# Unit 0's two chunks share one sine-table window: a new issue order for all engines of a fused gated-attention and MoE kernel

## The chip, the cores and the metric

One core of one Trainium2 chip runs the whole program in one launch. The metric is the device time of one execution in microseconds, median of a few runs. The core has five engines that run side by side, each with its own instruction queue in strict order: PE (TensorE, matmuls), DVE (VectorE), ACT (ScalarE, which needs a table load before it may change between the log/exp functions and the sine functions), POOL (GpSimd) and SP (SyncE, here the only issuer of transfers). An instruction that waits blocks all that stand behind it in its engine's queue.

## The reference, cut to what matters

```python
def _attn_ref(q, k, v, a_re, a_im):            # (4, 8, 768, 48) each
    mag = np.sqrt(a_re * a_re + a_im * a_im)
    scale = np.minimum(mag, 0.999) / (mag + 1e-06)
    a_re_n, a_im_n = a_re * scale, a_im * scale
    for t in range(S):                         # complex decay of a state, per (b, h)
        S_re, S_im = a_re_n*S_re - a_im_n*S_im, a_re_n*S_im + a_im_n*S_re
        S_re = S_re + outer(k[t], v[t])
        y[t] = q[t] @ S_re
    return y

def _moe_ref(x, w_in, w_out):                  # x: 3072 x 384, d_ff 2048
    h = x @ w_in
    sp = log1p(exp(h))                         # h itself above 20
    return (h * np.tanh(sp)) @ w_out
```

The attention output, reshaped to 3072 rows of 384, is the input `x` of the second part.

## The kernel before

**Units and chunks.** The 4 x 768 time steps are cut into 12 units of 256 steps (`UNITS`), each with two chunks of 128 (`NCH`). The complex decay is written in polar form. For each unit ACT and DVE work out the log of the magnitude, add it up along time (a scan, L409), and take exps of plus and minus the sum (L413, L414); the angle goes through an arctan, a second scan (L426), a reduction to one turn (L431 or L432, then L433), and sines (L491). `grow` (L453) multiplies q and k by the exps, `turn1` and `turn2` (L475) by the sine and the cosine, and six transfers per chunk (`relay`, L471) bring the result into the layout of the matmuls (tile `T`). Then PE works on the chunk: transposes of k (`kn`, L561, copied out of PSUM at L562), the 128 x 128 products (`pa`, L597; from unit 3 on `pp`, L592) with their mask (L599), the output (`ypsum`, L612, copied at L617), and the state update (`pd`, L632, then L637 or L639 and L640). The output is moved by transfers (`xf<-y`) and split into a high and a low half (`xH`, `xL`, L255 and L256).

**The second part.** `mm1` (L695 for unit 0, L699 after) multiplies by `w_in` into `ph`, ACT and DVE make the activation (L703 to L709), its result is split into halves (L255, L256), and `mm2` (L732 for unit 0's early half, L736) multiplies by `w_out` into `po`. The weights are loaded as `raw` (SP, L277), converted by ACT (L285), DVE (L287, L288) and POOL (L290) and split into `w` (L255, L256).

**Warming matmuls.** `spin` (L525) issues 84 matmuls into `junk` whose results nobody reads; the first 40 wait for chunk 0's L433 (`turned`), the other 44 for the copy of chunk 0's output (`copied`).

**Order.** The functions are called in the order of a list of due times, which gives each engine a numbered list of instructions. `in_order` then chains them in the order that the table `ORDER` names: in `"Activation": "0 45 47 46 48+3 ..."` the number n is the n-th instruction of that engine in program order, and `48+3` means 48, 49, 50. `FLIP` lists which of 214 movable steps (copies out of PSUM, casts, one reduction step, two small column copies) go to their second engine, and `SETS` gives the number and kind of table loads (`l` log and exp, `t` sine and arctan). A table load is one more numbered ACT instruction, so `ORDER` alone says where it stands. Unit 0 is worked by chunks:

```python
for g in groups:
    steps += each(*(() if g else (size,)), slope, test, mag1, mag2, mag3, mag4, mag5, grow, gs=(g,))
    ...
    steps += [lambda g=g: window((g,)), lambda g=g: turn1(g), lambda g=g: turn2(g)]
```

PSUM tiles of the tag `pa` (`pkn`, `pa`, `pd` of units 1 and 2) share two buffers: a product in `pa` can start only when a transpose's buffer was copied out.

Of the kernel before, what the change touches and what calls it, by code (L numbers as in the profile page):

```python
# [115 lines left out]
    """,  # L116
    "DVE": """
# [72 lines left out]
FLIP = "0 3 5 8 10+2 16 23+3 27 29 31 34 41 43+2 46+6 53+3 57 60+2 63 65+4 70 76+2 81 87+3 92+2 96 98 100 103+6 111+7 119 122 131 135+3 139 142 144 146+2 149 151+3 157 159+3 165+2 169+2 172 175 177+5 184 188+2 191+2 194 196 200+2 203+2 206+4 213"  # L190
# [808 lines left out]
```

## Time and profile before

| what | value |
|---|---|
| median of 3 runs | 567.69 us (567.3 to 569.6) |
| profiled execution | 568.46 us |
| its span (first to last instruction) | 566.8 us |
| mean granted clock of PE | 0.998 |
| busy: PE, DVE, ACT, POOL | 541.2, 467.1, 473.5, 41.1 us |
| matmuls into `junk` | 84, 22.9 us busy |
| table loads | 45, 57.7 us busy |

Busy time is the union of an engine's instructions. The start times of a timeline are microseconds from the first instruction; matmuls overlap in the pipeline, so their pitch (the distance of two starts) is what one costs PE.

### The profile page before, as it was taken

What the parts mean: (1) busy time and instruction counts of PE and PEld (TensorE: products, weight loads), DVE (VectorE), ACT (ScalarE), POOL (GpSimd) and SP (SyncE); (2) the same over time, 40 slices, a digit from 0 to 9 for tenths busy, and PEclk for the clock granted to TensorE, in tenths of its full rate; (3) what the DMA queues carried; (4) which work ended last, traced back from release to release, by engine and by line L of the source; (5) the groups of instructions that cost most, each with busy time, mean ns of one, the idle gap of its engine ahead of it and who ended that gap; (6) DMA issues with size and microseconds to landing.
All of it is one profiled execution on the core that took longest, in us unless ns stands there. A gap on an engine that the chain in (4) does not pass through costs nothing.

```text
span 566.8 us, 14350 instructions
## 1 busy us (share of the span) xinstructions
PE 541.2 (95%) x5830; PEld 504.3 (89%) x5830; DVE 467.1 (82%) x766; ACT 473.5 (84%) x757; POOL 41.1 (7%) x50
## 2 busy tenths in 40 slices
PE   0987999999999999999999999999999999999997
PEld 0556877899999999999999999999999999999996
DVE  6989999999999999899997999687997776563643
ACT  7998999999999999899986998878877689554562
POOL 3122322322000000000000000000000000000000
PEclk9999999999999999999999999999999999999999
DMA  8686763924675738627447426536446414301000
GB/s 290 225 276 167 299 194 90 303 65 105 189 211 131 208 106 226 174 80 212 124 124 190 130 85 178 180 89 178 148 116 156 117 54 118 103 17 43 16 14 32
DMA packets 69063, 81.65 MB, mean 144 GB/s; under 512 B 6144, under 2 KB 60672, under 8 KB 68992
## 3 DMA queue, kind: packets, MB, share of 16 engines
q1 hardware_dynamic: 68992, 80.68, 49.0%
q8 instruction: 47, 0.77, 0.6%
q14 instruction: 24, 0.20, 0.1%
HBM read 45.51 MB, written 11.40 MB: 100 GB/s over the span
## 4 chain that ended last, share of the span: by engine, by line
PE 83%; DVE 6%; DMA 4%; ACT 3%; SPq 2%; issue 1%; DVEq 0%
PE ph L699 32%; PE po L736 31%; PE ypsum L612 7%; PE po L732 4%; PE pp L592 4%; PE pp L632 2%; ACT L239 1%; PE pa L597 1%; PE ph L695 1%; DMA T<-QK 1%; DMA I<-a_im 1%; SPq L471 1%; DVE X L475 1%; DMA T<-X 1%; DVE QK L453 1%
## 5 line engine op out<-in xcount | busy, mean ns | idle before, releaser
L699 PE MATMUL ph<-xH,w 128*128 128x256 f32 x1104 | 222.1, 286 | 0.4 <-DVE g L709 0.4
L736 PE MATMUL po<-w,gh 128*128 128x384 f32 x704 | 202.0, 339 | 0.0
L699 PEld LDWEIGHTS ph<-xH,w 128*128 128x128 f32 x1104 | 179.9, 190 | 3.8 <-issue 1.4
L699 PE MATMUL ph<-xL,w 128*128 128x256 f32 x552 | 156.1, 283 | 0.0
L736 PEld LDWEIGHTS po<-w,gh 128*128 128x128 f32 x704 | 129.6, 188 | 2.3 <-issue 1.7
L736 PE MATMUL po<-w,gl 128*128 128x384 f32 x352 | 118.5, 337 | 0.0
L699 PEld LDWEIGHTS ph<-xL,w 128*128 128x128 f32 x552 | 104.9, 190 | 0.9 <-issue 0.5
L709 DVE SCALAR_TENSOR_TENSOR g<-e,ph 128x512 f32<-128x512 f32 (+1 forms) x100 | 65.8, 659 | 39.1 <-ACT e L707 30.9
L705 ACT ACTIVATE e<-e 128x512 f32<-128x512 f32 (+1 forms) x100 | 60.4, 610 | 29.0 <-DVE e L704 28.9
L703 ACT ACTIVATE e<-ph 128x512 f32<-128x512 f32 (+1 forms) x100 | 57.2, 573 | 31.9 <-PE ph L699 23.0
L736 PEld LDWEIGHTS po<-w,gl 128*128 128x128 f32 x352 | 66.2, 188 | 0.0
L256 DVE TENSOR_TENSOR gl<-g,gh 128x512 fp32r<-128x512 f32 x88 | 60.2, 687 | 6.3 <-ACT gh L255 5.9
L707 ACT ACTIVATE e<-e 128x512 f32<-128x512 f32 (+1 forms) x100 | 60.6, 608 | 1.2
L706 ACT ACTIVATE e<-e 128x512 f32<-128x512 f32 (+1 forms) x100 | 60.2, 608 | 0.7
L239 ACT ACT_TABLE_LOAD x45 | 57.7, 1283 | 1.6 <-PEq L951 0.8
L704 DVE TENSOR_SCALAR e<-e 128x512 f32<-128x512 f32 (+1 forms) x100 | 40.6, 409 | 17.0 <-ACT e L703 16.8
L525 PE MATMUL junk<-cmask 128*128 128x512 bf16 x84 | 22.9, 407 | 15.5 <-DVE I L433 14.7
L290 POOL TENSOR_TENSOR raw<-raw 128x768 int32<-128x768 int32 x16 | 31.5, 1975 | 63.1 <-DVE raw L288 24.5
L255 ACT CAST gh<-g 128x512 fp32r<-128x512 f32 x47 | 28.7, 611 | 6.7 <-PE po L736 5.6
L593 DVE COPY_PREDICATED am<-tmask,pp 128x512 f32<-128x512 uint8 x36 | 26.4, 737 | 7.9 <-PE pp L592 7.8
L612 PE MATMUL ypsum<-T,S 96*48 96x128 f32 x320 | 32.5, 276 | 0.1
L525 PEld LDWEIGHTS <-cmask 128*128 128x128 bf16 x84 | 8.4, 104 | 24.6 <-issue 17.5
(106 smaller groups left out, 828.6 us busy)
## 6 DMA issues: line engine op xcount, KB each, us to landing
T<-X SPq DMA_DIRECT2D x72, 129.0 KB, 2.9
T<-QK SPq DMA_DIRECT2D x72, 129.0 KB, 3.4
raw<-w_in SPq DMA_DIRECT2D x8, 768.0 KB, 6.1
raw<-w_out SPq DMA_DIRECT2D x8, 768.0 KB, 7.2
kd<-vx SPq DMA_DIRECT2D x45, 128.0 KB, 2.8
kn<-kd SPq DMA_DIRECT2D x15, 384.0 KB, 3.3
V<-v SPq DMA_DIRECT2D x12, 384.0 KB, 6.5
out_dram<-o SPq DMA_DIRECT2D x24, 192.0 KB, 2.3
```

The lines of the kernel that those rows point to most:

```text
L239: nc.scalar.preload_act_table_set({"l": "natural_log_exp_and_others", "t": "trig_and_small"}[name])
L256: leng(out=lo, in0=src, in1=h.bitcast(F32), op=ALU.subtract)
L290: nc.gpsimd.tensor_tensor(hi, hi, lo, ALU.add)
L612: nc.tensor.matmul(py[64 * par:64 * par + D, i, :], lhs, rhs, start=n == 0, stop=first or n == 1)
L699: nc.tensor.matmul(ph[:, a, :], rows_in(parts[j][:, wp], kt, a), st[xp][:, kt, :], start=n == 0, stop=n == 8)
L703: act(e, ph, AF.Exp)
L704: nc.vector.tensor_scalar_min(e, e, math.exp(20.0))
L705: act(e, e, AF.Square, bias=1.0)
L706: act(e, e, AF.Ln, scale=0.2, bias=0.2)
L707: act(e, e, AF.Exp, scale=-1.0)
L709: nc.vector.scalar_tensor_tensor(g, e, 2.5, ph, ALU.subtract, ALU.mult)
L736: nc.tensor.matmul(po[t], gp[:, a, tsl], rows_out(parts[NPAIR + j][:, wp], a), start=j in starts and a == 0 and n == 0, stop=j + 1 in ends ...
```

## The change

Only the tables differ; no function is edited. Read through the numbering above, they say this.

- **ACT, unit 0.** Before, the queue goes: log/exp table; the logs and exps of chunk 0 (and two early steps of chunk 1); sine table; arctans and sines of chunk 0; log/exp table; logs and exps of chunk 1; sine table; sines of chunk 1; log/exp table. After, it goes: log/exp table; logs and exps of chunk 0 and of chunk 1, and unit 1's squares, first log and first exp; sine table; arctans of chunk 0, unit 1 and chunk 1; sines of chunk 0; two conversions (L285); the reduction step and the sines of chunk 1; log/exp table. Two loads fewer there. Over the whole program `SETS` goes from 45 loads to 39.
- **DVE and POOL, unit 0.** The logs' DVE steps of chunk 1 now stand before chunk 0's scan of the angle; POOL does the small column copies of chunk 1 and chunk 0 in that order, then the conversions.
- **SP.** Ahead of chunk 0's relay now stand also a third weight load (`raw`, 768 KB) and unit 1's V; chunk 1's relay sends QK before X; unit 1's QK loads and chunk 0's `xf` transfers alternate; two `w_out` loads now stand between the relays of unit 1's two chunks.
- **PE.** 34 instead of 28 junk matmuls ahead of chunk 0's first transpose, 12 together between unit 0's last two products; 73 instead of 75 in all ahead of unit 1's first `pa`. There, unit 1's `pa` is followed by one `mm1` group and then the second `pa` (before: both `pa`, then the `mm1` group). Later, the order of the groups is new everywhere.
- **Engines of movable steps** (90 of 214 change): 29 casts go from ACT to DVE and 26 from DVE to ACT; 6 copies of `y` to DVE and 3 to ACT, among these chunk 0's (DVE before, ACT after) and chunk 1's the other way; of unit 1's first two `kn` copies the second goes from DVE to ACT, behind a table load and an arctan; 8 column copies from DVE to POOL and 4 back; 6 output copies to ACT and 3 to DVE. ACT has 746 instructions before and 736 after, DVE 738 and 738, POOL 47 and 51, PE 4333 and SP 384 in both.

```diff
 ORDER = {
     "PE": """
-        0+28 40+8 28 48+4 29+5 52+4 64+16 56+8 34 80 35 81+2 124+4 83+4 36 87+6 128+4 93+8 37 101+2 132+4 103+2 38 105+3
...
+        0+34 40+16 64+16 56+8 34+3 80 37 81+4 38 85 124+4 86+2 39 88+2 128+4 90+2 132+4 92+12 136+4 104+2 188+6 226+6
...
     "Activation": """
-        0 45 47 46 48+3 55 53+2 52 51 1 56 70 65 73 57+3 2 60+3 66 71 75 72 63+2 68 3 67 69 82 77 83 79 4 74 76 78 125+2
...
+        0 39 41 49 40 42+3 47 64 48 54 45 55 46 56 65 67 66 58 57 1 50 76 59 52 51 53 69 60 75 62 61 63 2 68 70+3 118+2
...
     "Pool": """
-        16 3 46 14 0 5+2 9 11 1 7 10 15 12 4 8 2 17+2 20 19 21+4 26 25 29 27+2 30+2 33 32 34+2 38 13 36+2 39 41 40 42+4
+        3 5 1 16 13 9 7 0 14 12 10 6 2 15 4 19 18 17 21 20 22+4 27 50 8 26 30 28 31 29 32+2 35 34 36+2 11 38+12
     """,
     "SP": """
-        0+4 8 17 16 7 5 4 46 9 11 18 6 19+5 47 15 10 26 24+2 29 27+2 12 14 13 44 42 45 43 48 51 31+2 30 33 36 38 37 35
...
+        0+2 3 2 16 8 17 4 6 46 5 9+3 7 15 19 18 23 20 22 21 12 29 27+2 24 26 25 47 14 45 13 44 43 42 48 51 31+2 30 33
...
-SETS = "l t l t l t l t l t l t l t l t l t l t l t l t l t l t l t l t l t l t l t l t l t l t l"
+SETS = "l t l t l t l t l t l t l t l t l t l t l t l t l t l t l t l t l t l t l t l"
```

## Rows read from the trace of the kernel before

**Rows 1.** The page: span, busy time, and two of its costliest groups (busy, mean ns).

```profile
span 566.8 us, 14350 instructions
PE 541.2 (95%) x5830; PEld 504.3 (89%) x5830; DVE 467.1 (82%) x766; ACT 473.5 (84%) x757; POOL 41.1 (7%) x50
...
L239 ACT ACT_TABLE_LOAD x45 | 57.7, 1283 | 1.6 <-PEq L951 0.8
L525 PE MATMUL junk<-cmask 128*128 128x512 bf16 x84 | 22.9, 407 | 15.5 <-DVE I L433 14.7
```

**Rows 2.** Busy time by stretch: length, then busy us of each engine.

```profile
10.00:20.00 10.00, 5.33 (x16) 2.09 (x17) 9.71 (x19) 9.81 (x17) 0.41 (x1) 1.00 0.71 241
...
80.00:120.00 40.00, 39.96 (x288) 31.75 (x287) 39.10 (x59) 39.58 (x60) 11.24 (x6) 1.00 0.60 183
```

**Rows 3.** ACT's timeline in the head: start us, us, instruction.

```profile
10.72 1.28 ACT L239 ACT_TABLE_LOAD   x1
...
20.84 0.83 ACT L377 ACTIVATE X<-X 128x768 f32<-128x768 f32 x1
21.57 0.51 ACT L413 ACTIVATE X<-R 128x384 f32<-128x384 f32 x1
21.99 0.51 ACT L414 ACTIVATE X<-R 128x384 f32<-128x384 f32 x1
...
38.61 0.84 ACT L491 ACTIVATE X<-I 128x768 f32<-128x768 f32 x1
...
54.80 0.84 ACT L491 ACTIVATE I<-I 128x768 f32<-128x768 f32 x1
```

**Rows 4.** DVE's timeline in the head.

```profile
13.96 0.56 DVE L433 SCALAR_TENSOR_TENSOR I<-X,I 128x384 f32<-128x384 f32 x1
...
15.78 0.96 DVE L475 TENSOR_TENSOR X<-QK,X 128x768 f32<-128x768 f32 x1
...
24.98 0.96 DVE L475 TENSOR_TENSOR X<-QK,X 128x768 f32<-128x768 f32 x1
...
30.08 0.68 DVE L617 COPY y<-ypsum 112x512 f32<-112x512 f32 x1
...
39.62 1.76 DVE L453 TENSOR_TENSOR QK<-QK,X 128x1536 f32<-128x1536 f32 x1 [1.33 <-DMA xf<-y]
...
42.65 1.75 DVE L475 TENSOR_TENSOR X<-QK,X 128x1536 f32<-128x1536 f32 x1
...
54.23 0.55 DVE L562 COPY kn<-pkn 128x384 f32<-128x384 f32 x1
```

**Rows 5.** PE's timeline in the head, with the wait ahead in brackets.

```profile
14.67 8.12 PE L525 MATMUL junk<-cmask 128*128 128x512 bf16 x28 [14.67 <-DVE I L433]
23.63 0.85 PE L561 MATMUL pkn<-ident,T 96*128 96x96 f32 x8 [0.84 <-DMA T<-QK]
...
33.17 2.54 PE L525 MATMUL junk<-cmask 128*128 128x512 bf16 x11
...
52.14 0.52 PE L561 MATMUL pkn<-ident,T 96*128 96x96 f32 x4 [1.40 <-DMA T<-QK]
...
54.84 2.05 PE L597 MATMUL pa<-T 96*128 96x128 f32 x16 [1.41 <-DVE kn L562]
56.73 1.58 PE L695 MATMUL ph<-xf,raw 128*128 128x128 f32 x12
58.23 1.07 PE L632 MATMUL pd<-V,kn 128*64 128x48 f32 x31
```

**Rows 6.** SP's transfer issues in the head.

```profile
34.09 2.58 SPq L653 DMA_DIRECT2D xf<-y  x4
```

**Rows 7.** The chain that ended last, 352 to 358 us: pieces on PE.

```profile
352.03 1.25 PE pp L592 x64
353.28 1.27 PE ph L699 x9
...
355.07 1.08 PE ph L699 x9
```

More of the change, by code (lines that the diff above doesn't have):

```diff
@@ L75 @@
     "PE": """
[40 rows of a table removed]
[40 rows of a table added]
     """,
     "DVE": """
[25 rows of a table removed]
[25 rows of a table added]
     """,
     "Activation": """
[24 rows of a table removed]
[23 rows of a table added]
     """,
     "Pool": """
-        16 3 46 14 0 5+2 9 11 1 7 10 15 12 4 8 2 17+2 20 19 21+4 26 25 29 27+2 30+2 33 32 34+2 38 13 36+2 39 41 40 42+4
+        3 5 1 16 13 9 7 0 14 12 10 6 2 15 4 19 18 17 21 20 22+4 27 50 8 26 30 28 31 29 32+2 35 34 36+2 11 38+12
     """,
     "SP": """
[13 rows of a table removed]
-    """,
-}
-FLIP = "0 3 5 8 10+2 16 23+3 27 29 31 34 41 43+2 46+6 53+3 57 60+2 63 65+4 70 76+2 81 87+3 92+2 96 98 100 103+6 111+7 119 122 131 135+3 139 142 144 146+2 149 151+3 157 159+3 165+2 169+2 172 175 177+5 184 188+2 191+2 194 196 200+2 203+2 206+4 213"
-SETS = "l t l t l t l t l t l t l t l t l t l t l t l t l t l t l t l t l t l t l t l t l t l t l"
[13 rows of a table added]
+    """,
+}
+FLIP = "0+2 3 5+2 9+2 14 19 23+2 27 31 34 43+2 46+5 53 55 57 59 61 65 67+2 70+2 74 79+4 84+2 89+2 93+2 97+2 100+8 109+5 115 117 120+2 123+4 128+2 131 133 135+3 142 145+2 148 150+2 153+4 158 160 162+6 172+2 177+4 183+2 186+2 189+2 192+5 198 201+4 207 211 213"
+SETS = "l t l t l t l t l t l t l t l t l t l t l t l t l t l t l t l t l t l t l t l"
 def in_order(tc, nc):
```

197 rows, old and new, of the table ORDER are left out of this document.

## The prediction

> **What bounds the kernel now.** I read the page first: PE is busy for 541.2 of 566.8 us [rows 1], so either PE's own work or what stands ahead of it sets the time. Then busy time by stretch: from 80 to 120 us PE is busy for 39.96 of 40 us, and ACT and DVE for 39.58 and 39.10 beside it [rows 2]. All three are full there, but PE is the one that has no gap. The head is different: from 10 to 20 us ACT has 9.81 and DVE 9.71 of 10, while PE has 5.33, and that is junk [rows 2, 5]. So the time is made of three pieces: a head in which ACT and DVE set the pace and PE mostly warms up; a long stretch in which PE works through a fixed list; a tail. The junk itself is 84 matmuls in both kernels. A change of order can then win in two ways only: PE reaches a given place of its list earlier at the end of the head, or the same list costs PE less because its groups follow each other differently.
>
> Where does the head end? PE's timeline shows it. The first real matmul waits for a transfer until 23.63; unit 1's first transpose waits for another until 52.14; unit 1's first `pa` waits until 54.84 for a copy on DVE [rows 5, 4]. Behind this last wait the matmuls stand shoulder to shoulder. I therefore follow the new order as far as unit 1's first state update, `pd` at 58.23 [rows 5]: ahead of it both kernels have the same real matmuls on PE, and behind it 9 junk matmuls are left in both. What `pd` gains there goes to the end.
>
> **Chunk 0 comes later.** Between ACT's first and second table load the new order puts five 384-column steps of chunk 1 and four 768-column steps of unit 1. Their pitches are 0.42 (21.57 to 21.99) and 0.73 us (20.84 to 21.57) [rows 3], so 5 x 0.42 + 4 x 0.73 = 5.0. The load moves from 10.72 to 15.7, the arctan to 17.0, and L433 on DVE from 13.96 to 19.0. The junk waits for L433: it starts at 19.7 instead of 14.67. 28 of them took 8.12; the six more cost 0.22 each (11 in 2.54, less one's own length) [rows 5], so PE is free for chunk 0's first transpose at 19.7 + 8.1 + 1.3 = 29.1. Its relay is ready before that: `turn1` at 15.78 + 5.0 = 20.8, and before it took 7.9 from there to the transpose at 23.63 [rows 4, 5], so 28.7. So the transpose is 5.5 us late.
>
> What is late next? The copy of the output `y`: before it ended at 30.76, 7.1 after the transposes began [rows 4, 5]. Six of the junk matmuls in between are gone (1.3 us), so it ends at 29.1 + 5.8 = 34.9; at best, if the wait on DVE's other work shrinks too, at 34.0. Before, the transfers of `y` went out only at 34.09 [rows 6], because SP's queue had other issues ahead of them. So 3.2 to 4.1 us of lateness meet a cover of 3.3 us, and the second part of chunk 0 starts about when it did. That cover is the reason why I charge nothing for it; without it, it would cost up to those 4.1.
>
> **Chunk 1 and unit 1.** Two loads are gone between chunk 0 and chunk 1: 2 x 1.283 = 2.57 us of ACT [rows 1]. Chunk 1's `turn1` was at 24.98 [rows 4]. It cannot gain all of it, since DVE must now first do both turns of chunk 0 (2 x 0.96) just ahead of it; between -2.57 and +0.5, I take -0.9. Unit 1's sine is bounded by a new wait: chunk 0's `y` copy now stands in ACT's queue, and behind it wait the second exp of unit 2's size, a conversion, unit 1's two exps, two `kn` copies, the reduction step and the sine load. With four 768-column steps at 0.73, the conversion at about the same, two copies at 0.42 or a little more and the load at 1.28 that is 5.8 to 6.0 behind 34.0 to 34.9. So the sine starts at 39.8 to 40.9, against 38.61 [rows 3], and `turn1` of unit 1 cannot start before 40.6. Before, it started at 42.65, four microseconds behind its sine, because `grow` ahead of it waited until 39.62 for a transfer [rows 3, 4]. So it may gain up to 2.0 or nothing; I take -0.7, nearer to nothing, for DVE's own scans have to follow chunk 0's late mask steps. Unit 1's relay keeps that, so its first transpose comes at 52.14 - 0.7 = 51.4.
>
> **The copy that PE waits for.** Before, unit 1's second `kn` copy was on DVE, 54.23 to 54.78, and both `pa` followed at 54.84 [rows 4, 5]. Now it is on ACT behind a table load and the arctan of unit 2. Before, that arctan ran at 54.80, 16.2 behind unit 1's sine [rows 3]; the list between the two has about the same steps and fewer waits on DVE, so I put it 14.0 (13 to 16.2) behind a sine at 40.3, at 54.3; with 0.84 for it and 0.4 for the copy, the copy ends at 55.5 (54.3 to 57.7). But the new order needs this copy only for the second `pa`: the first one takes the buffer of the other copy (which stands five ACT steps earlier), then comes the `mm1` group, then the second. So at 55.5 only one `pa` (2.05 / 2 = 1.0) and two junk (0.4) are left ahead of `pd`: 56.9, where before, from 54.84, two `pa`, the `mm1` group and `pd`'s place came to 58.23 [rows 5]. That is -1.3. Its bounds: -2.5 and +0.9 by the copy's two ends; if the first `pa` needs that copy too, it is +0.9 at the middle value already (rival a).
>
> **PE's list.** Behind a group of small tiles (`pp`, `ypsum`) the next full-size group costs more: `ph` x9 took 1.27 behind `pp` and 1.08 elsewhere [rows 7], 0.19 each. Read from the two orders, PE goes from such a group to `ph` or `po` 33 times before and 29 times after: -0.76. Against it, it changes between `pp` and `ypsum` 14 times instead of 8, which no row here prices; if each cost as much, +1.1. I take -0.8 + 0.1 = -0.7, since those two both run in small tiles; the ends are -0.8 and +0.4.
>
> **The other edits.** Four fewer loads later on (5.1 us of ACT), the flips of casts and copies (DVE's count does not change), four more column copies on POOL (busy for 41.1 of 566.8 [rows 1]): nothing, because PE is full there [rows 2] and covers them; without that cover the loads would give 5.1. The tail has the same last steps on each engine: nothing. The sum is -1.3 - 0.7 = -2.0. The profiled execution took 568.46, 0.77 above the median of the runs; against it this gives 566.5, against the median 565.7.
>
> [...]
>
> **The rivals.** (a) The copy on ACT holds both `pa`. Then `pd` comes at 55.5 + 2.05 + 1.5 + 0.2 = 59.2, +0.9, and with PE's list -0.7 the kernel is at 567.9. For it: before, the first `pa` did wait for that very copy and not for the one that ended earlier [rows 5]. Against: the buffers are given out in the order in which they come free, and the new order puts the `mm1` group between the two `pa`. (b) Slower: chunk 0's relay lands late. Its transfers now stand behind 1.15 MB more. At the 241 GB/s of that stretch [rows 2] this is 4.8 us, and the `raw` behind it, if it runs beside it, 3.2 more. Up to a landing at 29.1 the junk hides it; from there ACT, which waits for the `y` copy, hands on each microsecond to unit 1's sines and to `pd`. With 4.8 the kernel is at 565.7 + 28.7 + 4.8 - 29.1 = 570.1, with both at 573.3; from a landing 0.4 us later than the first of these it is slower by over 0.5%. Against it: the DMA engines were busy for only 0.71 of that stretch [rows 2], and the added loads stand in SP's queue ahead of the relay's wait, so they go out while ACT still works on the logs. (c) The saved loads count in full: 6 x 1.283 = 7.7, so 560.0. Only if ACT sets PE's pace; against it stand PE's 39.96 of 40.
>
> **How the numbers follow.** A measurement of this kernel can tell about 0.5%, 2.8 us, from no change. My forecast has 0.65: 565.7, its own range 563.3 to 567.5; as it ends 0.8 above the bound of "faster" (564.9), 0.27 of the 0.65 lie below that, 0.38 inside. (a) has 0.13, all inside. (b) has 0.17, 0.13 of it slower and 0.04 inside. (c) has 0.05, faster. So faster 0.32, same 0.55, slower 0.13. The range goes from the early end of the copy with unit 1's `turn1` at its early end too (565.7 - 1.2 - 2.0 = 562.5) to (b) with the extra bytes alone: 562.5 to 570.1.
>
> **What would show it.** Table loads at about 15.7 and 24 in the head, junk from 19.7, chunk 0's first transpose at 29, its `y` copy at 34 to 35 with ACT idle ahead of it for 1 to 2 us, unit 1's `turn1` near 42, the second `kn` copy near 55.5, `pd` of unit 1 near 57, and from there no gap on PE. I am wrong if `pd` comes at 58 or later, if PE shows gaps of over 1 us in all behind it, or if the lists of `ph` and `po` are not 0.7 shorter.

## The result and the profile after

The kernel got slower: 573.48 us (median of 6 runs, 571.4 to 575.09) against 568.0 (6 runs, 567.3 to 569.6), a ratio of 1.0089 with an interval of 1.0061 to 1.0117. The forecast was 565.7 with a range up to 570.1: wrong, and on the other side. The order table is one line shorter, so every line number behind it is one smaller (L699 of before is L698 here).

The page answers [rows 1]: span, busy time, and the groups of the junk and of the table loads.

```profile
span 569.9 us, 14345 instructions
PE 541.6 (95%) x5830; PEld 502.9 (88%) x5830; DVE 467.0 (82%) x766; ACT 464.6 (82%) x747; POOL 40.2 (7%) x54
...
L238 ACT ACT_TABLE_LOAD x39 | 50.0, 1283 | 1.5 <-PEq L950 0.8
L524 PE MATMUL junk<-cmask 128*128 128x512 bf16 x84 | 23.2, 417 | 19.6 <-DVE I L432 19.6
```

ACT has 7.7 us of loads less, and PE does the same work in the same time (541.6 us against 541.2), but the span is 3.1 longer. So the loss is waiting of PE, not work. The profiled execution took 571.59 us, one of the two fastest of the six; it shows 3.1 of the 5.5 us.

The head went nearly as forecast. ACT's timeline answers [rows 3] (the last `kn` copy is the one for which the forecast let the second `pa` wait); PE's answers [rows 5].

```profile
15.62 1.28 ACT L238 ACT_TABLE_LOAD   x1
...
24.47 1.28 ACT L238 ACT_TABLE_LOAD   x1
...
34.13 0.58 ACT L616 COPY y<-ypsum 112x512 f32<-112x512 f32 x1 [1.58 <-PE ypsum L611]
...
55.97 0.46 ACT L561 COPY kn<-pkn 128x384 f32<-128x384 f32 x1
```

```profile
19.56 10.10 PE L524 MATMUL junk<-cmask 128*128 128x512 bf16 x34 [19.56 <-DVE I L432]
29.50 0.83 PE L560 MATMUL pkn<-ident,T 96*128 96x96 f32 x8
...
52.91 1.13 PE L596 MATMUL pa<-T 96*128 96x128 f32 x8
...
55.28 1.06 PE L596 MATMUL pa<-T 96*128 96x128 f32 x8
...
56.70 1.07 PE L631 MATMUL pd<-V,kn 128*64 128x48 f32 x31
```

`pd` comes 1.5 us earlier than in [rows 5]. The two waits of 1.40 and 1.41 us ahead of it there are gone; the second `pa` starts at 55.28, ahead of the `kn` copy at 55.97, so neither `pa` waited for that copy. Where the loss stands is seen in busy time by stretch (length, then busy us of PE, PEld, DVE, ACT, POOL). After:

```profile
60.00:120.00 60.00, 59.35 (x452) 46.96 (x451) 58.49 (x88) 56.96 (x96) 17.69 (x13) 1.00 0.65 201
120.00:240.00 120.00, 118.15 (x1402) 113.82 (x1402) 114.43 (x183) 112.36 (x176) 6.26 (x11) 1.00 0.58 163
240.00:360.00 120.00, 117.97 (x1410) 113.19 (x1405) 101.74 (x163) 102.48 (x165) 0.21 (x1) 1.00 0.52 147
360.00:520.00 160.00, 160.00 (x1895) 154.99 (x1894) 117.69 (x199) 117.31 (x190) 0.41 (x2) 1.00 0.37 103
```

From 60 to 520 us PE is idle for 0.65 + 1.85 + 2.03 + 0 = 4.53 us; the same windows of the kernel before sum up to 459.47 busy of 460, 0.53 idle:

```profile
sum 460.00, PE 459.47 PEld 434.56 DVE 394.29 ACT 395.84 POOL 24.40; mean PE 114.87 PEld 108.64 DVE 98.57 ACT 98.96 POOL 6.10
```

4.0 us more waiting, less 1.3 of idle time ahead of 60 us (19.56 against 20.84), and 0.4 more of busy time (the junk alone took 0.3 longer) make the 3.1; behind 520 us the idle time is the same.

PE's waits in that time, by what ended them (engine, tile, line, releaser: us in total, times, longest):

```profile
PE po L735 <- DVE gl L255: 1.6, 1, 1.6
PE ph L698 <- DVE g L708: 1.1, 3, 0.4
PE pp L591 <- DMA T<-QK: 0.9, 1, 0.9
PE ph L698 <- DVE I L424: 0.5, 1, 0.5
PE pa L596 <- ACT kn L561: 0.4, 1, 0.4
```

They end at 63, 80, 138, 191, 197, 270 and 356 us. One of them (80 us, 0.26) has another cause, which is told below as theory E. The other six end on a landing, or on a step of DVE or ACT whose queue had just stood still for one.

What DVE and ACT waited for is told in the same way by the waits that a landed transfer ended. After, and then the kernel before:

```profile
DVE vx L569 <- DMA T<-QK: 2.2, 1, 2.2
DVE vx L569 <- DMA T<-X: 2.2, 2, 1.3
DVE xH L254 <- DMA xf<-y: 1.9, 1, 1.9
DVE xH L254 <- DMA out_dram<-o: 1.3, 1, 1.3
DVE g L708 <- DMA held<-o: 0.7, 1, 0.7
...
ACT xH L254 <- DMA kd<-vx: 1.6, 1, 1.6
ACT X L374 <- DMA xf<-y: 0.8, 1, 0.8
```

```profile
DVE xH L255 <- DMA xf<-y: 1.1, 1, 1.1
DVE xL L256 <- DMA T<-X: 0.9, 1, 0.9
DVE vx L570 <- DMA T<-QK: 0.5, 1, 0.5
...
ACT xH L255 <- DMA xf<-y: 1.5, 3, 0.8
```

With one or two of under 0.5 us it is 11.0 us against 4.4. Not each of them costs time: the third row is a wait at 391 us, and from 360 to 520 us PE has no idle time. The first row is the clearest place: unit 3's transpose `vx` (L569) needs all six pieces of the relay `T`. SP, DVE and PE there:

```profile
184.60 0.60 SPq L470 DMA_DIRECT2D T<-QK  x1
185.38 0.47 SPq L576 DMA_DIRECT2D kn<-kd  x1
185.89 0.55 SPq L470 DMA_DIRECT2D T<-QK  x1
```

```profile
188.30 0.68 DVE L708 SCALAR_TENSOR_TENSOR g<-e,ph 128x512 f32<-128x512 f32 x1
191.21 1.24 DVE L569 STREAM_TRANSPOSE vx<-T 96x1024 f32<-96x1024 f32 x1 [2.23 <-DMA T<-QK]
```

```profile
191.13 0.76 PE L591 MATMUL pp<-T 96*32 96x128 f32 x32 [0.92 <-DMA T<-QK]
```

SP puts out an issue every 0.6 us here (14 from 179.58 to 188.34). The last piece of this chunk goes out at 185.89, behind pieces of the next chunk and behind `kn`, and the transpose starts 5.3 us later; DVE had come to it at 188.98 and stood for 2.23 us. All of DVE's queue stood behind it, and PE waited 0.92 here and 0.52 at 197, where a late `g` (L708) and the short step L424 behind it end at 197.2 and 197.3. In the kernel before the last piece of `T` went out at 184.2, the second of the first row below, and the transpose stood at 189.16, without a wait:

```profile
183.62 1.19 SPq L471 DMA_DIRECT2D T<-QK  x2
...
189.16 1.23 DVE L570 STREAM_TRANSPOSE vx<-T 96x1024 f32<-96x1024 f32 x1
```

### The profile page after: what moved, and what is told of

Read it like the earlier page. It is cut to its first block, busy times and chain, and to the rows that moved or that the text cites. A ratio compares the mean times of both kernels' runs of the same rounds, so it can differ in the third digit from the quotient of the medians.

```text
span 569.9 us, 14345 instructions
## 1 busy us (share of the span) xinstructions
PE 541.6 (95%) x5830; PEld 502.9 (88%) x5830; DVE 467.0 (82%) x766; ACT 464.6 (82%) x747; POOL 40.2 (7%) x54
## 4 chain that ended last, share of the span: by engine, by line
PE 69%; ACT 12%; DMA 7%; DVE 6%; SPq 3%; issue 2%; DVEq 0%; ACTq 0%
PE po L735 28%; PE ph L698 28%; PE ypsum L611 5%; PE pp L591 4%; DMA T<-QK 2%; ACT L238 2%; PE junk L524 2%; PE pp L631 2%; SPq L470 1%; DMA xf<-y 1%; DMA QK<-q 1%; ACT e L706 1%; ACT e L705 1%; ACT w L254 1%; ACT raw L284 1%
## 5 line engine op out<-in xcount | busy, mean ns | idle before, releaser
L698 PE MATMUL ph<-xH,w 128*128 128x256 f32 x1104 | 224.3, 288 | 1.6 <-DVE g L708 1.1
L698 PEld LDWEIGHTS ph<-xH,w 128*128 128x128 f32 x1104 | 180.1, 190 | 6.6 <-issue 2.8
L698 PE MATMUL ph<-xL,w 128*128 128x256 f32 x552 | 156.0, 283 | 0.0
L698 PEld LDWEIGHTS ph<-xL,w 128*128 128x128 f32 x552 | 104.8, 190 | 1.4 <-issue 0.8
L708 DVE SCALAR_TENSOR_TENSOR g<-e,ph 128x512 f32<-128x512 f32 (+1 forms) x100 | 65.9, 659 | 24.3 <-ACT e L706 22.9
L704 ACT ACTIVATE e<-e 128x512 f32<-128x512 f32 (+1 forms) x100 | 60.8, 609 | 25.8 <-DVE e L703 25.7
L255 DVE TENSOR_TENSOR gl<-g,gh 128x512 fp32r<-128x512 f32 x88 | 59.8, 684 | 4.4 <-ACT gh L254 4.1
L705 ACT ACTIVATE e<-e 128x512 f32<-128x512 f32 (+1 forms) x100 | 60.7, 609 | 1.3
L703 DVE TENSOR_SCALAR e<-e 128x512 f32<-128x512 f32 (+1 forms) x100 | 41.1, 414 | 22.6 <-ACT e L702 22.5
L524 PE MATMUL junk<-cmask 128*128 128x512 bf16 x84 | 23.2, 417 | 19.6 <-DVE I L432 19.6
L289 POOL TENSOR_TENSOR raw<-raw 128x768 int32<-128x768 int32 x16 | 28.5, 1787 | 66.6 <-DVE raw L287 28.5
L254 ACT CAST gh<-g 128x512 fp32r<-128x512 f32 x45 | 27.3, 609 | 3.5 <-DVE g L708 3.0
```

Source lines behind the costliest of these rows:

```text
L255: leng(out=lo, in0=src, in1=h.bitcast(F32), op=ALU.subtract)
L524: ins = nc.tensor.matmul(junk, cmask, cmask.unsqueeze(1).broadcast_to([P, 4, P]), start=True, stop=True)
L698: nc.tensor.matmul(ph[:, a, :], rows_in(parts[j][:, wp], kt, a), st[xp][:, kt, :], start=n == 0, stop=n == 8)
L703: nc.vector.tensor_scalar_min(e, e, math.exp(20.0))
L704: act(e, e, AF.Square, bias=1.0)
L705: act(e, e, AF.Ln, scale=0.2, bias=0.2)
```

## The experiments

The theories that the expectations name. **A**: the new order puts steps of DVE and ACT that a transfer feeds where the landing has no slack; all that is queued behind them waits, PE last. **B**: the 90 movable steps that change their engine load DVE or ACT where PE needs them. **C**: the new head makes later transfers or buffers late. **D**: PE's own list got longer. **E**, formed on the way: a step of DVE is held while an add on POOL runs, and that takes the head's gain. All runs, with the ratio to the kernel before on the same chip, PE's idle time from 60 to 520 us in the profiled execution, and the waits on landings in DVE and ACT from 55 to 520:

| kernel | median us | ratio (interval) | profiled us | PE idle | landings |
|---|---|---|---|---|---|
| before | 568.0 | | 568.46 | 0.53 | 4.4 |
| after | 573.5 | 1.0089 (1.0061 to 1.0117) | 571.59 | 4.53 | 11.0 |
| again | 574.1 | 1.0112 (1.0078 to 1.0145) | 574.98 | 7.31 | 13.3 |
| head_new | 568.5 | 1.0010 (0.9991 to 1.0030) | 568.50 | 1.89 | 5.7 |
| head_old | 574.1 | 1.0101 (1.0071 to 1.0132) | 574.42 | 7.09 | 11.9 |
| flips_255 | 571.9 | 1.0082 (1.0048 to 1.0116) | 573.75 | 2.94 | 3.4 |
| sp_fix | 569.2 | 1.0016 (0.9993 to 1.0038) | 570.43 | 4.88 | 7.7 |
| act_fix | 571.9 | 1.0067 (1.0041 to 1.0093) | 571.68 | 5.31 | 9.8 |
| both_fix | 569.8 | 1.0038 (1.0017 to 1.0059) | 568.24 | 3.41 | 4.0 |
| late | 570.9 | 1.0065 (1.0039 to 1.0091) | 568.42 | 2.14 | 7.8 |
| head_dve | 570.2 | 1.0045 (1.0022 to 1.0069) | 570.95 | 3.22 | 4.7 |
| second | 566.9 | 0.9975 (0.9961 to 0.9989) | 565.98 | 0.85 | 4.8 |
| head_dve2 | 567.3 | 0.9986 (0.9972 to 1.0000) | 568.59 | 2.55 | 6.0 |
| old_second | 569.5 | 1.0032 (1.0013 to 1.0050) | 567.89 | 1.08 | 3.4 |

**again** is the changed kernel once more, without an edit.

> The changed kernel once more, for another profiled execution. Theory A (the new order puts steps on DVE and ACT that need a landed transfer where the landing has no slack, and everything queued behind them waits, PE last): 571 to 575 us, and behind unit 1's first state update PE again loses 3 to 8 us in single waits, each ending on a step that a transfer feeds, their sizes different from those of the first profile. Theory D (PE's own list got longer, by its order of groups): the same time, but single waits of under 1 us in all and longer pitches between groups.

574.1, and 7.31 us of PE idle, most of it at the places of the first profile (64, 141, 194, 200 and 273 us there), and some at new ones: at 121 PE stood 1.4 us for what was queued behind a conversion of a weight (L284), which had waited 2.0 us for its load. So single executions differ by how late their landings are, as A has it. D falls: it expected less than 1 us of single waits.

**head_new, head_old**: the new head with the old order behind it, and the other way round. The first, against the kernel before (every engine's list is after's up to its last start ahead of 57 us, then before's without those):

```diff
-SETS, 45 loads; FLIP = "0 3 5 8 10+2 16 23+3 27
+SETS, 43 loads; FLIP = "0+2 3 5+2 9+2 14 23+3 27
 "PE": """
-        0+28 40+8 28 48+4 29+5 52+4 64+16 56+8 34 80 35
+        0+34 40+16 64+16 56+8 34+3 80 37
```

> The new order and engines for all that starts before 57 us, the order of the kernel before behind it. Theory A: the head is worth what the profile of after showed, -1.5 us, and nothing is lost behind it: 566.5 against 568.0. Theory C (the new head leaves transfers or buffers late, and the loss behind it comes from that): 570 or more. If the head gains nothing that lasts: 568.0.

> The order and engines of the kernel before for all that starts before 58.6 us, the new order behind it. Theory A: the loss lies in the new order behind the head, and the head's 1.5 us are missing too: 573 to 575. Theory C: with the old head the loss goes away, 568 or below.

568.5 and 574.1: the whole loss is in the order behind the head, so C falls. But the head's 1.5 us did not last either. In head_new's profile `pd` starts at 56.53, 1.7 us earlier than in [rows 5], and by 91 us PE has lost 1.2 of that again, in two waits (0.49 and 0.74). The first, by DVE, POOL and PE (line numbers are one larger than before's):

```profile
76.15 2.27 DVE L257 TENSOR_TENSOR xL<-xf,xH 128x768 fp32r<-128x768 f32 x1
```

```profile
76.14 1.46 POOL L291 TENSOR_TENSOR raw<-raw 128x768 int32<-128x768 int32 x1
```

```profile
78.80 0.39 PE L700 MATMUL ph<-xH,w 128*128 128x256 f32 x1 [0.49 <-DVE g L710]
```

The step of DVE took 2.27 us instead of 0.95: POOL's add had started 0.01 us ahead of it, and it ended 0.82 us behind the add's end, about its own length. Theory E comes from here.

**flips_255**: the order of before, and 55 casts (L255) change their engine.

```diff
-FLIP = "0 3 5 8 10+2 16 23+3 27 29 31 34 41 43+2 46+6 53+3
+FLIP = "0 3 5 8 10+2 16 23+2 27 29 31 34 43+2 46+6 53 55
```

> The order of the kernel before, in which only the 55 casts of L255 that the change moves between ACT and DVE change their engine, each put into the other queue at the time at which it started before. Theory A: the engines are not the cause, 567.5 to 569. Theory B (the new engines overload DVE or ACT at places where PE needs them): 570 or more.

571.9, which is what B expected. It does not show B for the changed kernel, though: the waits on landings are 3.4 us here, less than before, and PE's idle time is 2.94, with waits that end on steps of DVE, `g` and `o` above all. The larger part of the profile's loss is PE's busy time, 544.2 us against 541.2 [rows 1], and there the clock fell, at 54 to 58 us (the column behind POOL's, as a share of full speed):

```profile
50.00:54.00 4.00, 1.80 (x15) 1.26 (x13) 4.00 (x6) 3.20 (x7) 3.21 (x1) 1.00 0.86 238
54.00:58.00 4.00, 3.38 (x19) 3.38 (x20) 2.90 (x7) 3.96 (x6) 0.37 (x1) 0.68 1.04 310
```

So this kernel loses about as much as the whole change (1.0082 against 1.0089), but what of it the casts cost and what the clock is not separated; whether they cost something in the new order is decided by a kernel that keeps them (second, below).

**sp_fix, act_fix, both_fix** leave the engines as in after and move issues of SP forward (the numbers are SP's), or two steps of ACT back, or both.

```diff
 "SP": """
-        90 108
+        90 93 108
...
-        129 146 142 139 143 130 141 152
+        129 142 143 141 146 139 130 152
...
-        199 210 202 213 214 201 192
+        199 202 201 210 213 214 192
 "Activation": """
-        112 167 100 104 98
+        112 100 104 167 98
...
-        191 196 177 185
+        191 177 196 185
```

> The changed kernel with eight transfer issues moved forward in SP's queue, each by a few places, at the five places where the two profiles of it show DVE or ACT waiting for a landing: the store of a held output (138 us), unit 3's relay T for vx (191), the last transfer of xf for two units (270 and 355), a relay piece at 250. Queues of PE, DVE, ACT and POOL are left alone. Theory A (late landings): the 4.7 us that PE loses behind them come back in large part, 569 to 571. Theory B (the engines to which the change moves casts and copies are what holds PE): 573 or more, with the same waits of PE at other releasers.

> The changed kernel with two steps that a transfer feeds moved back in ACT's queue: the square on a_re (62 us) behind the kn copy and an exp that stood behind it, and the conversion of weight 15 (113 us) behind the cast of weight 12. SP's queue is left alone. Theory A: a step with a late landing costs those that stand behind it, so 0.6 to 1.0 us come back at the first place and up to 1.5 at the second, where an execution has that wait: 572 to 573.5. Theory B: 574.

> The two edits above together. Theory A: 567.5 to 570, the time of the kernel before or somewhat behind it, and a spread of single executions that is narrower. Theory B: 573 or more.

Eight issues moved by a few places give 4.3 to 4.9 us back (569.2 against 573.5 and 574.1): A. The wait of `vx` at 191 us is gone; the four pieces of `T` go out together and the transpose follows without a gap:

```profile
182.13 2.51 SPq L470 DMA_DIRECT2D T<-QK  x4
```

```profile
188.35 1.23 DVE L569 STREAM_TRANSPOSE vx<-T 96x1024 f32<-96x1024 f32 x1
```

The profiled execution (570.43, above the median) still has 4.88 us of PE idle, at other places and no less than the 4.53 of after: what the edit gives is shown by the times, not by this pair of profiles. The largest of PE's waits:

```profile
PE pp L631 <- DMA kn<-kd: 2.5, 2, 1.3
```

At the first of its two places (190 us) `kn` goes out at 185.45, as in after (185.38), where the same `pp` started at 189.33 without a wait; here it started at 190.04. So this landing took longer with the same issue time; why, no run shows. act_fix gave 1.6 to 2.2, somewhat more than expected, but its interval overlaps that of after. Both together lie in the range of A (569.8) but gave no more than SP's part alone, and single executions spread over 5.6 us where those of after spread over 3.7: the narrower spread that was expected did not come.

**late** is the counter-test: the kernel before with three issues of SP moved back.

```diff
 "SP": """
-        127 141 143
+        127 143
-        145 130
+        145 141 130
...
-        211 199 208
+        211 208
...
-        269 266 283
+        269 283
```

> The kernel before, in which three transfer issues of SP's queue are moved back by a few places: the last transfer of xf for one unit (issue 262.1 to about 266), one of unit 3's relay (183.6 to about 186), and the last of xf for another unit (344.7 to about 347). The queues of all engines are left alone. Theory A: by what the landings took before, the three steps that need them start 1.9, 2.0 and 2.8 us late and PE loses something over half of that, 571 to 572. If DVE and ACT have slack behind those steps, so that late landings are no cause: 568 to 568.5.

570.9, 0.1 below A's range. No other engine's list was touched, and the three issues cost 0.65%. The profiled execution was its fastest (568.42) and shows one of the three late landings: ACT's `xH` at 349 us waits 3.55 us for its `xf`, and PE's idle time is 2.14 us, not 0.53.

**head_dve, second.** head_dve tests E: DVE starts a long step ahead of POOL's add at both places. second adds to both_fix a second set of moves of the same kind, and those two of DVE. The two lists below are DVE's of head_dve and SP's of second.

```diff
 "DVE": """
-        91 92
+        91 150 92
...
-        116 127
+        116 123 127
```

```diff
 "SP": """
-        57 63 54 50
+        57 54 63 50
...
-        118 131
+        118 127 128 129 131
-        137 127 136 128 129 142
+        137 136 130 142
...
-        261 282
+        261 256 282
```

> The new head with the order of before behind 57 us, and two steps of DVE moved forward: L388 between the cast xH and its difference xL (76 us), and the first L475 of unit 2 ahead of a step L704 (87 us). In the new head's profile these two places held a DVE step for 1.3 us each beside an add on POOL that had started 0.01 to 0.06 us ahead of it, and PE lost 0.5 and 0.75 there, which is what the head had gained. Theory E (these two collisions take the head's gain): DVE's long step now starts first and POOL's add waits instead, PE has no wait of over 0.4 us from 57 to 100 us, and the time is 566.5 to 567.2. If the gain is lost to something else: 568.5 as before the edit.

> The changed kernel with the forward moves on SP and the two on ACT, and a second set of the same kind: four issues of unit 3's and one of unit 8's kd and kn, one of xf (58 us) moved forward on SP, the conversion of weight 15 moved back by three more steps, and the two moves of DVE of the kernel beside this one. The waits that were left on PE in the profile before these edits came to 3.8 us (64, 94, 118, 190 and 343 us). Theory A: 566 to 568, below the kernel before or level with it. If the rest of the loss is not from landings and collisions: 569.5.

second: 566.9, 1.1 us below the kernel before and 6.6 to 7.2 below after, with all of after's engines and loads: A holds, and B is not what made after slow. It is the best version. head_dve went the other way, 570.2. The first move worked (no wait of PE at 78 us); the second did not:

```profile
86.98 1.76 DVE L476 TENSOR_TENSOR X<-QK,X 128x1536 f32<-128x1536 f32 x1
88.64 1.70 DVE L705 TENSOR_SCALAR e<-e 128x512 f32<-128x512 f32 x1
```

```profile
87.14 2.91 POOL L291 TENSOR_TENSOR raw<-raw 128x768 int32<-128x768 int32 x1 [7.56 <-DVE raw L289]
```

POOL's add started 0.16 us behind L476, as meant, and took 2.91 us for its 1.46, 1.31 of them behind the end of L476; L705 stood beside it for 1.7 us all the same and ended at 90.3, in head_new at 89.2. PE waited 2.2 us for the `g` behind it, and the clock granted to it was 0.83 in the stretch from 90 us (1.00 in the ten us before):

```profile
90.00:100.00 10.00, 8.55 (x33) 5.95 (x34) 7.58 (x12) 8.62 (x15) 1.19 (x2) 0.83 0.57 163
```

In second the same steps stand in the same order (the add at 85.92, 0.17 us behind L474), and there the short step, L703, took its usual 0.42 us and the add 3.25: which of the two takes longer differs between these profiles.

**head_dve2, old_second.** head_dve2 keeps the first of these moves and has, at the second place, steps ahead that read PSUM. old_second is second with the old head.

```diff
 "DVE": """
-        91 92
+        91 150 92
...
-        116 127 109 122 123
+        116 109 122 127 123
```

> The new head with the order of before behind 57 us, L388 between xH and xL as in the run before, and at the second place (87 us) no long step first: instead the copy o and the product g, which read PSUM and were not held beside POOL in any profile, stand ahead of the step L704. Theory E: PE's waits at 78 and 91 us are under 0.4 each, the head keeps its gain, 566.5 to 567.3. If the head's gain is lost in other places: 568.5.

> The kernel with all moves of the last set, but with the old head (order and engines of the kernel before for all that starts before 58.6 us). Its time against 566.9 is what the new head is worth once the landings no longer cost. By the profile of the changed kernel: 1.5 us more, 568.4. If the head is worth nothing there, 566.9; by the saved loads (two in the head, 2.6 us) at most 569.5.

head_dve2: 567.3, 1.1 us below head_new, at the upper end of what E expected. At 76 us its rows are:

```profile
75.55 0.95 DVE L389 SCALAR_TENSOR_TENSOR X<-R,X 128x768 f32<-128x768 f32 x1
...
76.43 0.95 DVE L257 TENSOR_TENSOR xL<-xf,xH 128x768 fp32r<-128x768 f32 x1
```

The second collision is gone too. That the time falls with both speaks for E, but not strongly: the intervals of head_new and head_dve2 touch, and the profile of head_dve2, above its median, has other waits (2.55 us of PE idle). old_second: 569.5, so behind the new head the repaired order is 2.6 us faster than behind the old one, more than the 1.5 read from the profiles; the last section says where the rest is. In front of the order of before the new head gives 0.5 (head_dve2).

## Why the prediction was wrong

**The step that failed** is the sentence on the other edits: "nothing, because PE is full there [rows 2] and covers them". I weighed the table loads, the flips and the column copies by their work, and found cover for it. I never priced the change of SP's order and of DVE's and ACT's places against it behind the head, though the diff rewrites all five lists. A full PE shows that nothing was late in the kernel before; it does not show by how much each landing was early. The cover was a few microseconds at some places and none at others: in the kernel before unit 3's last relay piece left 5.0 us ahead of its transpose, which was enough, and in after 3.1, where the transpose could start only 5.3 behind the issue. For the `xf` whose cast stood still at 267 us (the row whose wait the profile puts down to a store, `out_dram<-o`; with sp_fix, which moves that `xf` forward, it is gone) it was 6.0 us before and 3.6 after. This term, 0 in the sum, measured +4.0 us of PE waiting in the profiled execution of after and +6.8 in that of again.

**The head** was right in most of its steps: loads at 15.6 and 24.5 (15.7 and 24), junk from 19.6 (19.7), the transposes of chunk 0 at 29.5 (29.1), its copy at 34.13 with ACT idle for 1.58 (34 to 35, 1 to 2), the `kn` copy ending at 56.4 (55.5), `pd` at 56.70 (56.9). Unit 1's `turn1` came at 42.54, 0.1 earlier and not 0.7. Rival (a) did not happen: the first `pa` started at 52.91, ahead of that copy. But the wait on which the term of -1.3 was built did not happen either: the second `pa` started ahead of that copy too, and PE has no idle time from 20 to 57 us. That `pd` came within 0.2 of the forecast is luck. And the size of the term hung on one profile of before. Its `pd` at 58.23 was a late one: three other profiles with the old head and the same engines have 56.34, 56.36 and 56.89, nine with the new one 55.69 to 56.70. With these the gain at `pd` is nearer to half a microsecond than to 1.5. What the head does to the granted clock, the forecast did not have at all (last section).

**PE's list** was put at -0.7 for fewer changes from small-tile to full groups. PE's busy time did not fall (541.6 against 541.2 [rows 1], the junk's 0.3 included), and the matmuls of `ph` and `po`, added up one by one, take 700.8 us against 698.7. No gain is seen; that the added changes between `pp` and `ypsum` ate it was not tested.

**Rival (b)** had the right mechanism, a late landing behind other issues, at the wrong place: chunk 0's relay landed in time. That its 573.3 lies near the 573.5 measured is chance. **Rival (c)**: ACT has 7.7 us of loads less, and the time shows nothing of it in after.

**What I named as the test**, gaps of over 1 us in PE behind the head, is what the profile shows. With the landings repaired the kernel is at 566.9 where I had 565.7, but that does not bear the sum out: second holds moves that the change does not have, and what it gains on the kernel before may be the clock alone (last section).

## What to carry to other kernels

When a change rewrites the order of in-order queues, list for each step that a transfer feeds the time from the last issue to the step, before and after, beside the landing time that the trace shows; a step whose margin falls below it holds its whole queue, and can then hold an engine that was full before. A new order can be worth keeping: here eight issues moved forward gave back 4.3 us of 5.5, and some ten more moves took it below the kernel before. And a term read from one profiled execution wants a second execution, or another kernel with the same stretch, before it is trusted to a microsecond.

## What the runs showed of the hardware

**DVE and POOL.** Steps of DVE that start behind the start of an add on POOL (L290), by as little as 0.01 us, can take 1.2 to 1.3 us longer than usual: L256 2.27 us for 0.95 (after, head_new; in both it ends 0.82 us behind the add), L704 1.65 for 0.42 (again), L426 2.25 for 0.95 (old_second). Where DVE starts first, the single add of POOL takes 1.47 to 3.63 us in the kernel before and 1.47 to 2.18 in after; in the longest of them, at 49.80 us of the kernel before, a step of DVE that starts behind it still takes its usual time (L383 at 51.13 us, 0.95 us). Steps of DVE that read PSUM take no longer beside an add than elsewhere in these two profiles: 0.66 to 0.69 us (L599), 0.68 to 0.69 (L617), 0.54 to 0.55 (L639), 0.66 to 0.69 (L709 with 512 columns). What a plan can't fix is who is first: with 0.01 to 0.2 us between them, L256 was held in the first profile of after and not in the second, and L704 in the second and not in the first.

**The clock.** Of 89 runs of the kernel before, the 20 with a mean granted clock of 0.998 or more have a median of 566.6 us, the 57 at 0.996 to 0.997 have 568.0, and the 12 at 0.995 or less 569.6. The kernels with the old head mostly run at 0.996 to 0.998 (median of their runs), those with the new head at 0.999 to 1.0, but for head_dve with its long wait. From 50 to 54 us PE is busy for 2.02 of 4 us in the profile of before, where the clock held (1.00 there and in the 4 us behind), and for 4.00 in that of second:

```profile
50.00:54.00 4.00, 2.02 (x17) 1.48 (x15) 4.00 (x7) 2.80 (x7) 3.43 (x1) 1.00 0.84 224
```

```profile
50.00:54.00 4.00, 4.00 (x33) 3.10 (x32) 3.98 (x8) 3.78 (x7) 0.15 (x1) 1.00 1.01 309
```

In flips_255, with 1.80 of 4 there, the granted clock was 0.68 in the next 4 us, and `pd` came at 59.60. In old_second the clock fell, to 0.57, at another gap of the old head: PE is busy for 1.96 of 4 us from 28 to 32 us, and 11 junk matmuls in the 4 us behind take 3.64 us, in the kernel before 2.54 [rows 5]:

```profile
32.00:36.00 4.00, 4.00 (x15) 1.97 (x13) 3.94 (x7) 3.04 (x5) 0.00 (x0) 0.57 0.95 307
```

In the other three profiles with the old head (before, late, head_old) it held, at 1.00. From 20 to 57 us PE is idle for 3.6 to 6.5 us in these five and for 0 to 1.0 in the nine with the new head, and in none of the nine did the clock fall there. So a stretch at a lower granted clock (0.68, 0.57) stood behind a gap of the old head in two profiles of five, and none stood there with the new head; how often it does so can't be seen without a profile of each execution, only guessed from the means. It is likely most of what is left of the 2.6: between the profiles of old_second and second PE's busy time falls by 2.4 us (542.7 to 540.3), its idle time does not. It may also be all that second gains on the kernel before: its 12 runs all have a mean of 0.998 or more and a median of 566.9, and the 20 of the kernel before with such a clock have 566.6. The clock was not tested alone.

**What stays open.** The engine moves other than the 55 casts were not tried alone, nor was SP's whole order exchanged between the two kernels. How the 5.5 us of after are shared among the single places differs between executions and was not separated.
